# A22 T4 by Strassen once more in a convolution and hard-swish kernel, with its sums, signs and tiles rearranged

## Chip, core and metric

The kernel runs on one core of one Trainium2 chip. The metric is the device time of one execution, in microseconds; before the change it is 2399.19 us, the median of 3 runs (2398.7 to 2399.26).

## What is computed

```python
def _attn_ref(x, weight):                  # x (8, 4096, 192), weight (8, 7)
    w = softmax(weight, axis=-1)           # a weight for each head and tap
    x_pad = zeros of 6 rows in front of x
    out[b, s, h*24+g] = sum_k w[h, k] * x_pad[b, s + k, h*24+g]

def _moe_ref(x, w_in, w_out):              # w_in (192, 2048), w_out (2048, 192)
    h = x @ w_in
    relu6 = np.clip(h + 3.0, 0.0, 6.0)
    g = h * relu6 / 6.0
    return (g @ w_out).astype(np.float32)
```

The 8 x 4096 tokens that leave the causal convolution go through the two products; everything is float32 on the chip.

## The kernel before, in words

**Blocks.** The tokens are cut into 32 blocks of 1024, each of them two groups of N = 512 tokens. Block 0 is done plainly (`out_direct`), the last by `out_last`, and the 30 between by an h phase (`h_phase`) and an output phase (`out_strassen`). The loop stands at the end of the kernel. The order of the work on each engine is the order in the source (`manual_schedule`); every engine takes its own instructions in turn, and the waits between engines follow from the tiles that they read and write.

**Convolution.** Seven taps for a block's next neighbour, each one DVE instruction on 128 partitions x 1536 elements: the lower 64 partitions hold one token group, the upper 64 the other (`conv_units`, L271 the first tap, L275 the six others). They are issued at the start of the output phase. `swap` copies the halves across by two DMAs on SP (`OWN` and `OTHER` of tile `y`), and `y_sums` (L296) makes four sums for the Strassen form of the first product.

**h phase.** Four units of two halves. The plans `FIRST`, `SECOND` and `OTHERS` write out the order of PE's 88 matmuls (L323, 64 rows each; a float32 matmul is two instructions) and of the steps that follow: copies on ACT (L408, L411), the adds of p5 on DVE (L415, steps `AF` and `AD`), the relu on ACT (L329) and the gate on DVE (L333), which writes g. `X` in the first plan is the last store of the block before.

**g and its quarters.** g lies as A11, A21, A12, A22: half of the 2048 hidden features by token group. A11 and A12 are group 0, A21 and A22 group 1. After each unit POOL makes S3 = A11 - A21 (L517, 128x1024) and issues a DMA that adds A22 to A21 in place, which gives S1 (L443), and four sums of A11's quarters for the second level of Strassen (`a11_sums`, L537, 128x256 each, in tile `sums`).

**Output phase.** The seven products of Strassen's form (Winograd's variant, `prod`) are run in groups of four 32-column matmuls side by side, one PSUM bank to a group:

- `a11_round`: the first two 32-column pieces of A11 B11 by seven half products of 256 tokens (L545), beside its third piece and pieces of A12 B21 (L456). Two PSUM banks. Its results are put together by a copy on ACT and seven adds of 32x256 on DVE, with scratch tile `mp`.
- `three(4, 2, 1)`: A22 T4 (three pieces) and one of A12 B21.
- `rest_of_2` (L598): what is left of A12 B21, four matmuls of 512 tokens and four of 256.
- `three(7, 5, 0)`, `three(6, 5, 1)`, `three(3, 5, 2)`: S3 T3, S2 T2 and S4 B22, with the pieces of S1 T1.

Between them DVE has, in this order: the convolution's seven taps, the adds of `a11_round`, S2 = S1 - A11 in A11's place (L517, two instructions of 128x2048), the adds of the rest, S4 = A12 - S2 in A12's place (L517, two more), the sums of the results, transposes into `xt` (L647) and `y_sums`. SP stores the transposed rows and loads x for a later block. The six result tiles and `mp` (pool `cs`) and `xt` (pool `ot`, four buffers) have SBUF of their own. PSUM banks are taken and given back in turn (`take`, `give`).

**Weights.** At the start, POOL makes the sums of the weights (`w_sums`, L222), among them T1 to T4 of w_out and, in `w_q`, four sums of B11's quarters.

Of the kernel before, what the change touches and what calls it, by code (L numbers as in the profile page):

```python
# [16 lines left out]
def kernel(  # L17
# [7 lines left out]
):  # L25

# [127 lines left out]
    w_q = cst.tile([P, 4, UNITS, QS], F32, name="w_q")  # L154
# [64 lines left out]
    def w_sums():  # L219

        def sub(out, x, y):
            nc.gpsimd.tensor_tensor(out=out, in0=x, in1=y, op=ALU.subtract)  # L222

        for o, x, y in ((T1, B12, B11), (T3, B22, B12), (T2, B22, T1), (T4, T2, B21)):
            sub(w_out[:, :, o], w_out[:, :, x], w_out[:, :, y])
        y11, y12, y21, y22 = (
            w_out[:, c::2, B11, q * QS : (q + 1) * QS] for c in range(2) for q in range(2)
        )
        t1, t2, t3, t4 = (w_q[:, j] for j in range(4))
        for o, x, y in ((t1, y12, y11), (t3, y22, y12), (t2, y22, t1), (t4, y21, t2)):  # L230
            sub(o, x, y)
        b11, b12, b21, b22 = (w_in[:, c::2, s] for s in range(2) for c in range(2))
        t1, t2, t3, t4 = (w_in_t[:, j] for j in range(4))
        for o, x, y in ((t1, b12, b11), (t3, b22, b12), (t2, b22, t1), (t4, b21, t2)):
            sub(o, x, y)
# [24 lines left out]

    def conv_units(i, parts, cuts=1):


        x = x_tiles.pop(i)
        W = N // cuts

        def tap(part, k, t):
            c = c_sb[:, k : k + 1]
            to = y[:, part, t : t + W]
            if k == 0:  # L270
                nc.vector.tensor_scalar(  # L271
                    out=to, in0=x[:, part, t : t + W], scalar1=c, scalar2=None, op0=ALU.mult
                )
            else:
                nc.vector.scalar_tensor_tensor(  # L275
                    out=to, in0=x[:, part, k + t : k + t + W], scalar=c, in1=to,
                    op0=ALU.mult, op1=ALU.add,
                )

        return [  # L280
            lambda part=part, k=k, t=t: tap(part, k, t)
            for part in parts for k in range(KC) for t in range(0, N, W)
        ]
# [28 lines left out]
    def give(b):  # L312
        free_banks.append(b)
# [14 lines left out]
    def relu(r6, h):  # L328
        nc.scalar.activation(r6, h, ACT.Relu, bias=half[:], scale=1.0 / 6.0)  # L329
# [48 lines left out]
    class Unit:  # L378
# [7 lines left out]
        def run(self, op):  # L386
            u, k, bank = self.u, self.k, self.bank

            def slot(c, s):
                return w_in[:, 2 * u + c, s]  # L390

            mms = {
                "P1": ("a", slot(0, 0), OWN), "P2": ("a", slot(0, 1), OWN + 1),
                "K11": ("a", slot(0, 2), OWN + 2), "P5": ("e", w_in_t[:, 0, u], YS1),
                "P6": ("b", w_in_t[:, 1, u], YS2), "P7": ("b", w_in_t[:, 2, u], YS3),
                "P4": ("b", w_in_t[:, 3, u], OTHER + 1), "K21": ("b", slot(0, 2), OTHER + 2),
                "P3": ("f", slot(1, 1), YS4), "K12": ("f", slot(1, 2), OWN + 2),
                "K22": ("d", slot(1, 2), OTHER + 2),
            }
            if op in mms:  # L400
                to, w, third = mms[op]
                first = op in ("P1", "P5")
                if first:
                    bank[to] = take()
                half_mm(k, bank[to], w, third, first, True, not first)
            elif op == "F1":
                bank["b"] = take()
                nc.scalar.copy(out=psum[:, bank["b"]], in_=psum[:, bank["a"]])  # L408
            elif op == "CE":
                self.p5 = p5s.tile([P, N], F32, name="p5")  # L410
                nc.scalar.copy(out=self.p5[:], in_=psum[:, bank["e"]])  # L411
                give(bank["e"])
            elif op in ("AF", "AD"):
                to = bank[op[1].lower()] = take()
                nc.vector.tensor_tensor(  # L415
                    out=psum[:, to], in0=psum[:, bank["b"]], in1=self.p5[:], op=ALU.add
                )
            elif op[0] == "R":
                r6 = self.r6[op[1]] = rs.tile([P, N], F32, name="r6")
                relu(r6[:], psum[:, bank[op[1]]])  # L420
            else:
                group, c = self.results[op[1]]
                b = bank[op[1]]
                gate(g_of(2 * u + c, group, k), self.r6[op[1]][:], psum[:, b])
                give(b)

    def h_phase(left):
        work = {(u, k): Unit(u, k) for u in range(UNITS) for k in range(2)}
        for u, plan in enumerate(PLANS):
# [9 lines left out]
            if u:  # L439
                slots = slice(2 * u - 2, 2 * u)  # L440
# [5 lines left out]
            if u < UNITS:  # L446
                a11_sums(u)
# [32 lines left out]
    def out_direct(i, work):  # L480

        parts = [(k, q) for k in range(G) for q in range(G * NQ)]
        for r in range(0, len(parts), 4):
# [17 lines left out]
            xt = ot.tile([P, N], F32, name="xt")  # L501
            nc.vector.transpose(out=xt[:], in_=bank)
# [4 lines left out]
    def g_sums(engine, which, slots, width):  # L507

        forms = {
            3: (S3, A11, A21, ALU.subtract),  # L510
            2: (S2, S1, A11, ALU.subtract), 4: (S4, A12, S2, ALU.subtract),
        }
        for n in which:
            o, a, b, op = forms[n]
            for p in slots[::width]:
                r = slice(p, p + width)
                engine.tensor_tensor(out=o[:, r], in0=a[:, r], in1=b[:, r], op=op)  # L517

# [9 lines left out]
    X11, X12, X21, X22 = (A11[:, c::2, t : t + TH] for t in (0, TH) for c in range(2))  # L528

    def a11_sums(u):  # L530

        s1, s2, s3, s4 = (sums[:, n, u] for n in range(4))
        for o, a, b, op in (
            (s1, X21[:, u], X22[:, u], ALU.add), (s3, X11[:, u], X21[:, u], ALU.subtract),
            (s2, s1, X11[:, u], ALU.subtract), (s4, X12[:, u], s2, ALU.subtract),
# [17 lines left out]
    def a11_round(i, p1, p2):  # L553

        ba, bb = take(), take()
        a, b = (psum[:, n] for n in (ba, bb))
        y11, y12, y21, y22 = (
            w_out[:, k::2, B11, q * QS : (q + 1) * QS] for k in range(2) for q in range(2)
        )
        t1, t2, t3, t4 = (w_q[:, n] for n in range(4))  # L560
        s1, s2, s3, s4 = (sums[:, n] for n in range(4))
        m0 = (
            quarters(a, 0, first_half, X11, y11) + quarters(a, 0, second_half, X12, y21)
# [3 lines left out]
            quarters(a, 1, first_half, X22, t4)  # L567
            + quarters(a, 1, second_half, A12[:, ::2, first_half], w_out[:, ::2, B21, rows(2)])
            + quarters(b, 1, first_half, s1, t1) + quarters(b, 1, second_half, s4, y22)
        )  # L570
        m2, m3 = product(a, 2, 1, 2), product(a, 3, 2, 0)
        for n in range(NP):
            for mms, k in ((m0, 2 * n), (m1, 2 * n), (m2, n), (m3, n),
                           (m0, 2 * n + 1), (m1, 2 * n + 1)):
                mms[k]()
        mp = cs.tile([P, TH], F32, name="mp")
        r1, r2, r3 = (mp[rows(n)] for n in range(3))
        nc.scalar.copy(out=r1, in_=a[rows(0), first_half])
        piece(p1, 2, a, 2)
        piece(p2, 0, a, 3)  # L580
        add(p1[rows(0), first_half], r1, a[rows(0), second_half])
        add(r2, r1, b[rows(0), first_half])
        add(r3, r2, b[rows(0), second_half])
        add(p1[rows(0), second_half], r3, a[rows(1), first_half])
        add(p1[rows(1), second_half], r3, b[rows(1), first_half])
        add(r2, r2, b[rows(1), first_half])
        add(p1[rows(1), first_half], r2, b[rows(1), second_half])
# [3 lines left out]
    def rest_of_2(a):  # L591
# [3 lines left out]
        w = w_out[:, :, B21, rows(2)]  # L595
        for p, tokens in ((1, slice(0, N)), (0, second_half)):
            for j in range(4):
                nc.tensor.matmul(  # L598
                    out=bank[rows(j), tokens], lhsT=w[:, 2 * j + p],
                    rhs=A12[:, 2 * j + p, tokens], start=bool(p), stop=True,  # L600
                    tile_position=(0, j * QS), skip_group_check=True,
                )
# [40 lines left out]
    def store(i, c, k, half_, qs=range(NQ), queues=(nc.sync,), tokens=slice(0, N)):  # L643

        xt = ot.tile([P, N], F32, name="xt")
# [4 lines left out]

    def sums_tiles():
        return (cs.tile([DH, N], F32, name=f"c{k}") for k in range(6))
# [3 lines left out]
    def out_last(i):  # L656
# [19 lines left out]
        add(u2[:], p1[:], bank[m])  # L676
# [4 lines left out]
        add(p4[two], u3[two], p4[two], ALU.subtract)  # L681
# [7 lines left out]
        for t in range(0, N, N // 2):  # L689
# [9 lines left out]
            add(u3[rows(2), ts], u3[rows(2), ts], bank[rows(NQ), ts], ALU.subtract)  # L699
# [3 lines left out]
    def out_strassen(i, conv):  # L703
# [3 lines left out]
        ba, a = a11_round(i, p1, p2)  # L707
        g_sums(nc.vector, (2,), every, 4)
        b, bank = three(4, 2, 1)
        nc.scalar.copy(out=p4[:], in_=bank[m])  # L710
        piece(p2, 1, bank, NQ)
        give(b)
        swap(slice(0, K3))
        b, bank = rest_of_2(a)
        pieces(p2, 2, bank)
        give(b)
        add(p2[rows(2), first_half], p2[rows(2), first_half], a[rows(1), second_half])
        give(ba)
        g_sums(nc.vector, (4,), every, 4)
# [7 lines left out]
        add(u2[:], p1[:], bank[m])  # L727
# [3 lines left out]
        add(p4[:], u3[:], p4[:], ALU.subtract)  # L731
# [27 lines left out]
    with tc.manual_schedule():  # L759
# [115 lines left out]
        cs = ctx.enter_context(tc.tile_pool(name="cs", bufs=1))  # L875
        ot = ctx.enter_context(tc.tile_pool(name="ot", bufs=4))
# [8 lines left out]
        sums = ss.tile([P, 4, UNITS, N // 2], F32, name="sums")  # L885
        left = []
        for i in range(1, NB):
            h_phase(left)
# [39 lines left out]
```

## Time and profile before

| | |
|---|---|
| runs, median of 3 | 2399.19 us |
| the profiled execution | 2398.86 us |
| its span, first to last instruction | 2397.1 us |
| busy: PE | 2388.7 us (100%) |
| busy: DVE | 2138.0 us (89%) |
| busy: ACT | 1087.9 us (45%) |
| busy: POOL | 836.4 us (35%) |
| granted TensorE clock | 1.000 |
| PE L323 (h) | 884.8 + 524.5 us |
| PE L456, L545, L598 (products of the output phase) | 1120.0 + 218.9; 109.4 + 108.5 and two smaller forms; 31.6 and one smaller |
| DVE L275 (six taps), mean of one | 1786 ns over all shapes; 1922 ns for 128x1536 |
| DVE L271 (first tap), 128x1536 | 1806 ns |
| POOL L537 (sums of A11's quarters) | 188.1 + 101.9 + 90.3 us, 728 to 831 ns each |
| POOL L517 (S3) | 293.8 us, 2369 ns each |
| POOL's DMAs (L443) | 124 of 512 KB, 5.0 us from issue to landing |

A table of groups gives, for each source line and shape, how often it ran, for how long in all, and what the engine was waiting for before it. The order in time gives start, length, engine, line, operation, tiles and, in brackets, the idle time ahead. PE is TensorE's matmuls, PEld its weight loads, DVE is VectorE, ACT ScalarE, POOL GpSimd, SP the engine that issues most DMAs. PE's busy time is the union of overlapping matmuls, so the matmuls of one line share it with those beside them. Times within a block below are microseconds from the start of the span, in the block whose h phase runs from 1133.61 to 1171.83 and whose output phase from 1171.83 to 1207.62.

### The profile page before, as it was taken

Reading aid. Unit: us, or ns where it says so; the run is one execution under the profiler, and the core shown is the slowest. Engines: PE = TensorE matmul, PEld = TensorE weight load, DVE = VectorE, ACT = ScalarE, POOL = GpSimd, SP = SyncE. Lnnn points to the kernel's source line nnn. Section 1 sums busy time; section 2 is a strip of 40 time slices with the busy share of each in tenths; the row PEclk is TensorE's granted clock in tenths of the full one; section 3 lists DMA queues with packets and bytes.
Section 4 is the critical chain, followed back from the end, with each engine's and each line's share of the span. In section 5 each row is a group of like instructions: output and inputs, shape, how many; then the busy total and the mean of one; then the engine's idle time right before and its main releaser. Section 6 shows DMA issues by size and latency. Waiting matters only on the chain.

```text
span 2397.1 us, 43036 instructions
## 1 busy us (share of the span) xinstructions
PE 2388.7 (100%) x17496; PEld 1105.0 (46%) x17496; DVE 2138.0 (89%) x2773; ACT 1087.9 (45%) x1858; POOL 836.4 (35%) x780
## 2 busy tenths in 40 slices
PE   9999999999999999999999999999999999999998
PEld 6444444444444444444454444444444444444443
DVE  8798889988899988899888998889998889988896
ACT  7234553345543355433454334553445543455433
POOL 2524432234422344223443224432234422344222
PEclk9999999999999999999999999999999999999999
DMA  5233333323333233333333333333323233333322
GB/s 146 46 56 64 62 61 64 67 50 69 59 59 66 53 73 60 60 58 57 67 63 58 67 57 59 63 67 58 67 52 73 54 65 59 55 70 63 58 51 43
DMA packets 261143, 149.86 MB, mean 63 GB/s; under 512 B 207504, under 2 KB 212624, under 8 KB 260944
## 3 DMA queue, kind: packets, MB, share of 16 engines
q1 hardware_dynamic: 225880, 81.56, 16.9%
q0 software_dynamic: 33824, 65.28, 15.8%
q8 instruction: 137, 2.24, 0.4%
q14 instruction: 62, 0.51, 0.1%
q10 hardware_dynamic: 1240, 0.27, 0.1%
HBM read 31.72 MB, written 25.17 MB: 24 GB/s over the span
## 4 chain that ended last, share of the span: by engine, by line
PE 99%; DMA 0%; DVE 0%; SPq 0%; ACT 0%; issue 0%; DVEq 0%; ACTq 0%
PE psum L323 51%; PE psum L456 41%; PE psum L545 5%; PE psum L598 2%; DMA x<-in_x_dram 0%; DMA out_dram<-xt 0%; DVE c L641 0%; DVE xt L647 0%; SPq L106 0%; SPq L140 0%; DVE top L184 0%; PE psum L774 0%; DVE y L275 0%; SPq L95 0%; ACT y L788 0%
## 5 line engine op out<-in xcount | busy, mean ns | idle before, releaser
L456 PE MATMUL psum<-g,w_out 128*32 128x512 f32 (+1 forms) x7936 | 1120.0, 589 | 0.0
L323 PE MATMUL psum<-y,w_in 64*128 64x512 f32 x3664 | 884.8, 591 | 0.4 <-DVE y L275 0.3
L329 ACT ACTIVATE r<-psum,half 128x512 f32<-128x512 f32 x1024 | 641.0, 688 | 241.6 <-PE psum L323 234.8
L333 DVE SCALAR_TENSOR_TENSOR g<-r,psum 128x512 f32<-128x512 f32 x1024 | 641.7, 681 | 4.7 <-ACT r L329 1.5
L323 PEld LDWEIGHTS psum<-y,w_in 64*128 64x128 f32 x3664 | 441.6, 187 | 362.6 <-issue 292.2
L537 POOL TENSOR_TENSOR sums<-g 128x256 f32<-128x256 f32 x248 | 188.1, 831 | 1181.3 <-DVE g L333 1163.2
L456 PEld LDWEIGHTS psum<-g,w_out 128*32 128x32 f32 x7936 | 339.4, 110 | 460.3 <-issue 438.1
L323 PE MATMUL psum<-y,w_in_t 64*128 64x512 f32 x1984 | 524.5, 593 | 0.0
L415 DVE TENSOR_TENSOR psum<-psum,p 128x512 f32<-128x512 f32 x496 | 324.5, 694 | 193.1 <-PE psum L323 184.7
L633 ACT COPY c<-psum 32x512 f32<-32x512 f32 x218 | 126.0, 578 | 588.2 <-PE psum L456 571.0
L517 POOL TENSOR_TENSOR s<-g 128x1024 f32<-128x1024 f32 x124 | 293.8, 2369 | 245.5 <-PE psum L323 237.7
L275 DVE SCALAR_TENSOR_TENSOR y<-x,c_sb,y 128x1536 f32<-128x1536 f32 (+1 forms) x206 | 366.5, 1786 | 6.6
L323 PEld LDWEIGHTS psum<-y,w_in_t 64*128 64x128 f32 x1984 | 247.7, 186 | 195.2 <-issue 124.9
L517 DVE TENSOR_TENSOR g<-g 128x2048 f32<-128x2048 f32 x124 | 279.5, 2296 | 7.4 <-DMA g<-g 3.9
L456 PE MATMUL psum<-s,w_out 128*32 128x512 f32 x1488 | 218.9, 592 | 0.0
L408 ACT COPY psum<-psum 128x512 f32<-128x512 f32 x248 | 138.8, 571 | 71.7 <-PE psum L323 56.1
L443 POOL DMA_DIRECT2D g<-g x124 | 149.1, 1202 | 39.8 <-POOL s L517 39.8
L641 DVE TENSOR_TENSOR c<-c,psum 32x512 f32<-32x512 f32 (+2 forms) x219 | 139.8, 638 | 16.0 <-ACT c L633 9.7
L411 ACT COPY p<-psum 128x512 f32<-128x512 f32 x248 | 133.2, 591 | 41.1 <-PE psum L323 40.3
L456 PEld LDWEIGHTS psum<-s,w_out 128*32 128x32 f32 x1488 | 70.8, 110 | 129.2 <-issue 124.8
L545 PE MATMUL psum<-g,w_out 128*32 128x256 f32 x720 | 109.4, 380 | 0.0
L545 PE MATMUL psum<-sums,w_q 128*32 128x256 f32 x720 | 108.5, 379 | 0.0
(64 smaller groups left out, 1080.1 us busy)
## 6 DMA issues: line engine op xcount, KB each, us to landing
g<-g POOLq DMA_DIRECT2D x124, 512.0 KB, 5.0
out_dram<-xt SPq DMA_DIRECT2D x380, 64.0 KB, 2.0
y<-y SPq DMA_DIRECT2D x62, 384.0 KB, 4.7
x<-in_x_dram SPq DMA_DIRECT2D x55, 388.5 KB, 6.0
stage<-in_moe_w_in_dram SPq DMA_DIRECT2D x16, 192.0 KB, 4.4
stage<-in_moe_w_out_dram SPq DMA_DIRECT2D x8, 384.0 KB, 5.1
x<-in_x_dram SPq DMA_DIRECT2D x7, 384.0 KB
y<-y SPq DMA_DIRECT2D x6, 128.0 KB, 2.4
```

The lines of the kernel that those rows point to most:

```text
L275: nc.vector.scalar_tensor_tensor(out=to, in0=x[:, part, k + t : k + t + W], scalar=c, in1=to, op0=ALU.mult, op1=ALU.add,)
L323: nc.tensor.matmul(out=psum[:, b], lhsT=w[r], rhs=y[r, third_of_y], start=start, stop=stop, skip_group_check=onto,)
L329: nc.scalar.activation(r6, h, ACT.Relu, bias=half[:], scale=1.0 / 6.0)
L333: nc.vector.scalar_tensor_tensor(out=out, in0=r6, scalar=1.0, in1=h, op0=ALU.min, op1=ALU.mult)
L408: nc.scalar.copy(out=psum[:, bank["b"]], in_=psum[:, bank["a"]])
L415: nc.vector.tensor_tensor(out=psum[:, to], in0=psum[:, bank["b"]], in1=self.p5[:], op=ALU.add)
L443: nc.gpsimd.dma_start(out=S1[:, slots], in_=A22[:, slots], accum_op=ALU.add)
L456: lambda p=p: nc.tensor.matmul(out=bank[j * QS : (j + 1) * QS, tokens], lhsT=w_out[:, p, w, cols], rhs=x[:, p, tokens], start=(first and p ...
L517: engine.tensor_tensor(out=o[:, r], in0=a[:, r], in1=b[:, r], op=op)
L537: nc.gpsimd.tensor_tensor(out=o, in0=a, in1=b, op=op)
L545: lambda u=u: nc.tensor.matmul(out=dst[rows(j), tokens], lhsT=w[:, u], rhs=x[:, u], start=(u == 0 and tokens == first_half), stop=(u == UN ...
L641: nc.vector.tensor_tensor(out=out, in0=x, in1=y, op=op)
```

## The change

- **Products.** `a11_round` becomes `round_twice(n, ...)`, called twice: for A11 B11, and for A22 T4, whose first two pieces now go by seven half products as well. It takes the place of `three(4, 2, 1)`; its third piece and a piece of A12 B21 run beside it. The even half of A12 B21's last piece, second 256 tokens, moves into the second round, so `rest_of_2` keeps only its four 512-token matmuls.
- **Sums.** `quarter_sums(n, u)` makes for A22, too, four sums of 128x256 a unit on POOL; those of unit u - 1 stand ahead of that unit's S3 and S1 DMA. The last block makes none. `w_q` holds four more weight sums, of T4's quarters.
- **Signs.** The convolution's weights of group 1 are negated (`c_sg`), so h, A21 and A22 are; the relu of that group has scale -1/6. S3, S2 and S4 become sums, T1 changes sign, and some later adds and subtractions swap.
- **S2.** Since it is now a sum, its slots 0 to 3 are made by two adding DMAs from POOL; DVE makes slots 4 to 7 in one instruction.
- **First tap.** For every block but block 0 it is a multiplication on ACT.
- **Tiles.** Two tiles of 8 slots x 512 hold the sums of A11 and of A22; the six result tiles, `mp` and the four `xt` lie in slots of them.

```diff
         def tap(part, k, t):
-            c = c_sb[:, k : k + 1]
+            c = (c_sg if i else c_sb)[:, k : k + 1]
             to = y[:, part, t : t + W]
-            if k == 0:
+            if k == 0 and i:
+                nc.scalar.mul(to, x[:, part, t : t + W], c)
+            elif k == 0:
...
+        for n, block in enumerate((B11, T4)):
+            y11, y12, y21, y22 = (
+                w_out[:, c::2, block, q * QS : (q + 1) * QS]
+                for c in range(2) for q in range(2)
+            )
+            t1, t2, t3, t4 = (w_q[:, n, j] for j in range(4))
+            for o, x, y in ((t1, y12, y11), (t3, y22, y12), (t2, y22, t1), (t4, y21, t2)):
+                sub(o, x, y)
...
             if u:
+                if twice:
+                    quarter_sums(1, u - 1)
                 slots = slice(2 * u - 2, 2 * u)
                 g_sums(nc.gpsimd, (3,), range(NP)[slots], 2)
 
                 nc.gpsimd.dma_start(
                     out=S1[:, slots], in_=A22[:, slots], accum_op=ALU.add
                 )
-            if u < UNITS:
-                a11_sums(u)
+            if u < UNITS and twice:
+                quarter_sums(0, u)
...
-        mp = cs.tile([P, TH], F32, name="mp")
-        r1, r2, r3 = (mp[rows(n)] for n in range(3))
+        mp = tile_at(0, 2, P)
+        r1, r2, r3 = (mp[rows(k), first_half] for k in range(3))
...
+    def quarter_sums(n, u):
+
+        x11, x12, x21, x22 = (x[:, u] for x in quarter[n])
+        s1, s2, s3, s4 = (sums[n][:, j, u] for j in range(4))
         for o, a, b, op in (
-            (s1, X21[:, u], X22[:, u], ALU.add), (s3, X11[:, u], X21[:, u], ALU.subtract),
-            (s2, s1, X11[:, u], ALU.subtract), (s4, X12[:, u], s2, ALU.subtract),
+            (s1, x21, x22, ALU.add), (s3, x11, x21, ALU.subtract),
+            (s2, s1, x11, ALU.subtract), (s4, x12, s2, ALU.subtract),
         ):
             nc.gpsimd.tensor_tensor(out=o, in0=a, in1=b, op=op)
...
-    def rest_of_2(a):
+    def rest_of_2():
...
-        w = w_out[:, :, B21, rows(2)]
-        for p, tokens in ((1, slice(0, N)), (0, second_half)):
-            for j in range(4):
...
+        for j in range(4):
+            nc.tensor.matmul(
+                out=bank[rows(j)], lhsT=w_out[:, 2 * j + 1, B21, rows(2)],
+                rhs=A12[:, 2 * j + 1], start=True, stop=True, tile_position=(0, j * QS),
+            )
...
+    def tile_at(n, k, parts):
+        return sums_at[n][0:parts, k]
...
     def sums_tiles():
-        return (cs.tile([DH, N], F32, name=f"c{k}") for k in range(6))
+        return (tile_at(n, k, DH) for n, k in ((0, 0), (0, 1), (1, 0), (1, 1), (1, 2), (1, 3)))
+
+    xt_slots = [4, 6, 5, 7]
+
+    def next_xt():
+        xt_slots.append(xt_slots.pop(0))
+        return tile_at(1, xt_slots[-1], P)
...
-        ba, a = a11_round(i, p1, p2)
-        g_sums(nc.vector, (2,), every, 4)
-        b, bank = three(4, 2, 1)
-        nc.scalar.copy(out=p4[:], in_=bank[m])
-        piece(p2, 1, bank, NQ)
-        give(b)
+        ba, a = round_twice(0, first_half, p1, (1, 2, p1), (2, 0, p2))
+
+        for slots in (slice(0, 2), slice(2, 4)):
+            nc.gpsimd.dma_start(out=S2[:, slots], in_=S1[:, slots], accum_op=ALU.add)
+        g_sums(nc.vector, (2,), range(4, NP), 4)
+        bb, b = round_twice(1, second_half, p4, (4, 2, p4), (2, 1, p2))
         swap(slice(0, K3))
-        b, bank = rest_of_2(a)
+        b2, bank = rest_of_2()
         pieces(p2, 2, bank)
-        give(b)
-        add(p2[rows(2), first_half], p2[rows(2), first_half], a[rows(1), second_half])
+        give(b2)
+        for bank, tokens in ((a, first_half), (b, second_half)):
+            add(p2[rows(2), tokens], p2[rows(2), tokens], bank[rows(1), second_half])
         give(ba)
+        give(bb)
         g_sums(nc.vector, (4,), every, 4)
```

## Prediction

> **What bounds the kernel now.** I read first the page's chain that ended last (its shares by engine), then the busy times in the two stages of one steady block.
>
> ```profile
> PE 99%; DMA 0%; DVE 0%; SPq 0%; ACT 0%; issue 0%; DVEq 0%; ACTq 0%
> ...
> 1133.61:1171.83 38.22, 38.22 (x181) 21.91 (x177) 32.09 (x53) 27.73 (x47) 20.00 (x20) 1.00 0.36 66
> 1171.83:1207.62 35.79, 35.79 (x371) 13.50 (x369) 35.02 (x35) 5.68 (x11) 5.59 (x5) 1.00 0.30 57
> ```
>
> The columns of the last two lines are stretch, length, then PE, PEld, DVE, ACT, POOL busy. The first stretch is the h phase, the second the output phase; a block is 74 us, and there are 30 such blocks. PE never stops, so PE time saved is time saved. But in the output phase DVE is busy 35.02 of 35.79 us: it is a second bound, hidden only by its order. So I looked at when DVE delivers what PE needs. First DVE in the output phase, then PE's pieces of the block before (same lengths) from the chain in order of time:
>
> ```profile
> 1173.85 1.81 DVE L271 TENSOR_SCALAR y<-x,c_sb 128x1536 f32<-128x1536 f32 x1
> 1175.70 11.49 DVE L275 SCALAR_TENSOR_TENSOR y<-x,c_sb,y 128x1536 f32<-128x1536 f32 x6
> ...
> 1190.17 4.49 DVE L517 TENSOR_TENSOR g<-g 128x2048 f32<-128x2048 f32 x2
> ...
> 1197.31 4.50 DVE L517 TENSOR_TENSOR g<-g 128x2048 f32<-128x2048 f32 x2
> ...
> 1104.92 6.87 PE psum L456 x64
> 1111.79 1.29 PE psum L598 x16
> 1113.08 20.60 PE psum L456 x192
> ```
>
> The last L517 line is S4. Its first half ends at 1199.6 (half of 4.50 after 1197.31). The output phase ends at 1207.62, and its last product group (S4 by B22, the last third of the 20.60) takes PE 6.87, so it starts at 1200.75. S4 has 1.15 us to spare, and everything that DVE does after the h phase (seven taps, adds, S2, adds, S4) is queued ahead of it. That is the number on which this change turns.
>
> Third, POOL around the end of that h phase:
>
> ```profile
> 1167.15 2.35 POOL L517 TENSOR_TENSOR s<-g 128x1024 f32<-128x1024 f32 x1 [2.67 <-PE psum L323]
> 1169.80 1.20 POOL L443 DMA_DIRECT2D g<-g  x1 [0.30 <-POOL s L517]
> 1170.91 1.53 POOL L537 TENSOR_TENSOR sums<-g 128x256 f32<-128x256 f32 x2
> 1172.29 0.84 POOL L537 TENSOR_TENSOR sums<-sums,g 128x256 f32<-128x256 f32 x1
> 1173.21 0.73 POOL L537 TENSOR_TENSOR sums<-g,sums 128x256 f32<-128x256 f32 x1
> 1173.90 2.39 POOL L517 TENSOR_TENSOR s<-g 128x1024 f32<-128x1024 f32 x1
> 1177.28 1.20 POOL L443 DMA_DIRECT2D g<-g  x1 [0.98 <-POOL s L517]
> ```
>
> In each 9.45 us unit of the h phase POOL idles only about 2.7 us (the bracket), and its last S3 already reaches into DVE's taps. What that costs a tap (the first of these lines), and what POOL's weight sums at the start cost (the others):
>
> ```profile
> 1175.70 2.22 DVE L275 SCALAR_TENSOR_TENSOR y<-x,c_sb,y 128x1536 f32<-128x1536 f32 x1
> 1177.95 1.82 DVE L275 SCALAR_TENSOR_TENSOR y<-x,c_sb,y 128x1536 f32<-128x1536 f32 x1
> ...
> 70.58 3.27 DVE L275 SCALAR_TENSOR_TENSOR y<-x,c_sb,y 128x1536 f32<-128x1536 f32 x1
> 67.10 1.82 POOL L222 TENSOR_TENSOR w_out<-w_out 128x768 f32<-128x768 f32 x1
> 68.88 3.34 POOL L222 TENSOR_TENSOR w_out<-w_out 128x768 f32<-128x768 f32 x1
> ...
> 80.50 1.90 DVE L275 SCALAR_TENSOR_TENSOR y<-x,c_sb,y 128x1536 f32<-128x1536 f32 x1
> 84.72 0.46 POOL L222 TENSOR_TENSOR w_q<-w_out,w_q 128x128 f32<-128x128 f32 x1
> ```
>
> A tap is 1.82 us alone, 3.27 us beside 768-element POOL sums (which go from 1.82 to 3.34), 1.90 us beside 128-element ones. They take turns.
>
> **What the Trainium skill says.** "SBUF — State Buffer", section "SBUF: two separate sides": GpSimd and a DVE op with two SBUF inputs share a port pair as an exclusive lock held for the whole instruction; the loser blocks. The trace agrees: 3.27 against 1.82 us. Gates (one input in PSUM) are the same 0.68 us with or without POOL. "ScalarE: Activation LUTs", section "What ACT_TABLE_LOAD costs": 280 ns + 0.833 ns an element with a pointer operand, so 1.56 us for the moved tap; from the trace 1.59 us (a 128x512 one of the same kind is 0.723 us, and ACT copies of 256 and 512 elements, 361 and 578 ns, give 0.85 ns an element). "DMA: Bandwidth & Descriptors", section "SWDGE vs HWDGE vs iDMA": an accumulating DMA can only be issued from GpSimd, which is why S2's two stand behind POOL's sums.
>
> **The change, part by part.** All in the clock of this block.
>
> *Products (PE).* A22 T4's first two column pieces go by seven half products: the second round replaces the group of 6.87 us, and the four 256-token matmuls leave the remainder, 1.29 x 2/3 = 0.86, saves 0.43. Do 256-wide matmuls pay? In the round of today the 512-wide pairs beside them come every 0.429 us (16 pairs, 1172.30 to 1178.73 for 15 steps), as in the plain group (6.87/16): no; I take 0.02. Saved 0.41 us a block; at worst the round's whole excess of today, 7.03 - 6.87 = 0.16, comes again, and 0.27 is saved. On the path: 30 x 0.41 = 12.3 us.
>
> *A22's sums (POOL).* 4 units x 4 sums, 2.99 us a unit (1170.91 to 1173.90), into 2.7 us of idle: POOL falls behind. Walked from the first sum of the block (1142.63) with no idle left (units of 2.99 + 2.99, S3 and its DMA 3.79), A11's last sums end at 1174.8 instead of 1173.9. Then A22's last four and S3 (6:8) are still to come, 5.35 us of POOL's own time, all beside DVE's taps. Price of one on a tap: its own time less 0.37 (1.82 costs 3.27 - 1.82 = 1.45; 0.46 costs 0.08). So 4 x (0.72 - 0.37) + (2.36 - 0.37) = 3.4 us, against 0.40 today. Ends: 0.4 (nothing new; A22's sums then slip between) and 5.35 (all of it).
>
> *First tap on ACT.* ACT's last relu ends at 1173.2; 1.59 us; so tap 1 starts at about 1174.9, not 1175.70: DVE gains 0.80, not 1.81. The moved tap read one SBUF operand and was not held up by POOL; what moves forward is a tap that is. ACT is idle there (5.68 busy of 35.79): free. The new wait, tap 1 for ACT, has all of DVE's output phase queued behind it. Ends 0.6 to 0.95.
>
> *S2.* Half by DVE leaves 2.25 us of 4.49. The two DMAs stand on POOL behind S3 and the last S1 DMA: taps 1 to 4 with a sum each end near 1183.7, S3 near 1185.8, S1's DMA 0.98 later at 1186.8, landing (median 5.0) 1191.8; S2's follow at 1188.0 and 1189.2, landing 1193.0 and 1194.2, or 1194.8 and 1197.8 if each must take its 3.0 us alone (15.8% of 2397 us by 126 DMAs). Product 6 wants the first at 1193.5. DVE's own half of S2 waits for S1's landing (1191.8) and stands behind the conv, which ends at 1187.15 - 0.80 + 3.0 (the taps' loss, above) = 1189.4, and the first round's adds, 1192.4: no wait.
>
> *Adds (DVE).* Seven 256-adds as in round one, 3.04 us (the adds of L641 between the last tap at 1187.10 and S2 at 1190.17), and one more, 0.44. They share one scratch tile, so ACT's copy for the second round waits until DVE has read the first's (1192.4); behind it on ACT stand only copies that DVE wants later, and no relu for 15 us. SP's queue: the swap starts with the conv's end, 1189.5 instead of 1187.25, and lands 4.7 later, long before y_sums (after 1206): nothing.
>
> *The rest:* w_sums' four more small sums lie in the start, where POOL idles 18 us afterwards: nothing. Signs: nothing (same instructions). Result tiles in the sums' slots: each store's DMA lands in 2.0 us, the slot is written again over 20 us later: nothing. w_q and c_sg: two tiny instructions. PSUM banks: eight taken in turn, each given back before its next use.
>
> **The sum.** S4's first half: 1199.60 - 0.80 - 2.25 + 3.04 + 0.44 = 1200.03, with today's 0.40 of port loss; with 3.4, 1203.0. PE wants it at 1200.75 - 0.41 = 1200.34. So PE waits 2.7 (0.1 more for the signal) before its last group. The S1 and S2 landings lie under that wait: even 1197.8 for slots 2 and 3 puts the end of product 6 at 1197.8 + 6 x 0.86 = 1203.0. Next is late: DVE's first p5 add in the next h phase ends 12.16 us after S4's first half (1199.60 to 1211.76); PE needs it at its twelfth step, 6.87 + 11 x 0.433 = 11.6 us after it started that group. Another 0.5. A block: -0.41 + 2.8 + 0.5 = +2.9; x 30 = +87 on the profiled execution's 2398.86 us (span 2397.1; median of the runs 2399.19, 0.3 above): **2485**.
>
> **The rivals.** *Faster:* the port costs little, S4 comes in time, PE keeps 12.3 us: 2386.6. It decides at 0.3 us of port loss above today's 0.40 (1200.34 - 1200.03); with 0.7 gain and wait cancel. For it: total DVE work falls by under a microsecond. Against: 3.27 us taps in this very trace. *Slower still:* S2's landings, beside the swap's two DMAs at 1189.5 (4.7 us each), come 2 us later than 1197.8 and hold product 6: 2 x 30 more, 2545. *Doesn't do what it says:* if the second round costs the full 0.16, the gain is 8 us and the forecast 2489. *Milder:* if POOL keeps up and only S3 with one or two sums meets the taps (loss 2.0 to 2.4), the wait is 1.3 to 1.7 and the time 2440 to 2455.
>
> **Chances.** The DVE wait, its mild form and the full 0.16 included, 0.76 (2435 to 2520); late DMAs 0.08 (2520 to 2560); beyond 0.03; gain 0.10 (2386 to 2394); within 0.2% (4.8 us, about what can be told from no change) 0.03. Range 2435 to 2560 holds 0.84. Faster 0.10, same 0.03, slower 0.87.
>
> **What would show it.** Right: taps of about 2.4 us on average ((6 x 1.82 + 3.4)/6) instead of 1.92; PE waiting some 80 us in all for DVE's g (L517) at the product lines; blocks of 76.8 us; POOL without its 2.7 us brackets in the h phase. Wrong: taps still at 1.9; PE without waits; or PE waiting for the DMA on g.

## The result, and the profile after

The changed kernel takes **2643.84 us** (median of 4 runs, 2639.25 to 2649.55) against 2399.2 us, a ratio of 1.1021 [1.1, 1.1043]. The profiled execution took 2643.16 us (span 2641.3), granted clock 0.964. It is slower, as forecast, but by 245 us instead of 86, beyond the upper end of the range (2560).

Line numbers have moved: the products' matmuls are now L474, the second rounds L567, the six taps L290 and the moved tap L284, S3, S2 and S4 L535, POOL's quarter sums L559, S1's DMA L461, S2's DMAs L743, the swap L303 and L304. First the chain that ended last, by engine, of the kernel after:

```profile
PE 55%; POOL 24%; DMA 17%; issue 2%; DVE 2%; SPq 0%; POOLq 0%; ACT 0%; DVEq 0%; ACTq 0%
```

PE had 99% of it. Now 41% goes through POOL and DMAs, and DVE, which I had named as the bound to come, has 2%. Next the windows of one block: its h phase, its output phase, and two stretches within the latter (columns as in the prediction; the third number from the end is PE's granted clock, then the DMA share and GB/s):

```profile
1166.44:1204.52 38.08, 38.08 (x181) 20.33 (x177) 30.97 (x50) 27.79 (x47) 27.37 (x31) 1.00 0.33 60
1204.52:1250.13 45.61, 39.38 (x394) 15.43 (x392) 38.22 (x42) 7.51 (x13) 19.26 (x13) 0.93 0.42 73
1226.20:1236.00 9.80, 4.32 (x22) 0.92 (x26) 8.43 (x14) 0.58 (x1) 0.00 (x0) 0.81 0.89 162
1236.00:1243.30 7.30, 7.30 (x60) 1.99 (x56) 7.23 (x8) 0.00 (x0) 0.00 (x0) 0.79 0.12 19
```

The h phase is nearly what it was. The output phase is 45.61 instead of 35.79 us, and two things stand in it that no block of the kernel before had: 9.8 us in which PE is busy for 4.32 while the DMA engines are 89% busy, and a granted clock below 1. The mean block is 82.0 us (38.1 and 43.9) against 73.9.

The same output phase on DVE, POOL, PE, and then the DMA issues between 1218 and 1240 (the last number there is the median from issue to landing):

```profile
1207.38 14.51 DVE L290 SCALAR_TENSOR_TENSOR y<-x,c_sg,y 128x1536 f32<-128x1536 f32 x6 [0.76 <-ACT y L284]
...
1226.22 2.29 DVE L535 TENSOR_TENSOR g<-g 128x2048 f32<-128x2048 f32 x1 [1.30 <-DMA g<-g]
...
1235.56 4.49 DVE L535 TENSOR_TENSOR g<-g 128x2048 f32<-128x2048 f32 x2 [1.03 <-DMA g<-g]
```

```profile
1207.50 4.50 POOL L559 TENSOR_TENSOR sums<-g 128x256 f32<-128x256 f32 x2
...
1216.38 3.88 POOL L535 TENSOR_TENSOR s<-g 128x1024 f32<-128x1024 f32 x1
1220.57 1.20 POOL L461 DMA_DIRECT2D g<-g  x1 [0.30 <-POOL s L535]
1221.31 2.92 POOL L743 DMA_DIRECT2D g<-g  x2
```

```profile
1233.52 16.68 PE L474 MATMUL psum<-g,w_out 128*32 128x512 f32 x128 [5.48 <-DMA g<-g]
```

```profile
g<-g POOLq DMA_DIRECT2D x3, 512.0 KB, 12.2
y<-y SPq DMA_DIRECT2D x2, 384.0 KB, 8.6
```

DVE's taps take 14.51 us instead of 6 x 1.82 = 10.92, so they lose 3.6; the forecast was 3.4. POOL comes to S2's DMAs at 1221.31 and, by the trace, 1222.04, 16.8 and 17.5 us after the h phase; the forecast was 16.2 and 17.4. What is not as forecast is the landing. The first S2 DMA lands at 1233.5, 12.2 us after its issue, and PE stands 5.48 us for it. The second lands at 1235.5, and DVE's S4 waits 1.03 us for it. S1's last DMA, S2's two and the swap's two (SP issues them at 1221.95 and 1222.50) are in flight together. Over the whole run the waits of PE's products read (us in total, times, the longest):

```profile
PE psum L474 <- DMA g<-g: 167.2, 59, 6.1
```

That is 5.6 us a block; for DVE's g, where I expected 80 us, there is none.

The block above is one of seven in which POOL comes to the S2 DMAs at 16.8 us and they land within 2.4 us of each other. In 22 of the 30 blocks they leave about 2 us sooner, and PE stands twice, once for each of them, as here, where the output phase starts at 793.26:

```profile
818.27 2.73 PE L474 MATMUL psum<-g,w_out 128*32 128x512 f32 x16 [3.29 <-DMA g<-g]
823.25 13.60 PE L474 MATMUL psum<-g,w_out 128*32 128x512 f32 x112 [2.24 <-DMA g<-g]
```

In the mean of the 30 blocks the S2 DMAs are issued 15.4 and 16.1 us after the h phase and land at 25.9 and 30.2. After these waits PE runs at half clock in every block, for 3.41, 6.83 or 10.24 us (in one block twice 3.41), and the output phases last 41.9 to 45.6 us.

**Theory** after this reading: POOL's lateness makes S1 and S2 leave when the swap leaves; the five transfers share the 16 DMA engines; PE stands for S2, and the standing brings the half clock. **Rivals:** POOL's locks on DVE (my forecast) are the real cause and the DMA wait only covers it; the moved tap; S2 by DMA in itself; the second level of Strassen in itself.

### The profile page after: what moved, and what is told of

Its sections match the earlier page's. It is cut to its first block, busy times and chain, and to the rows that moved or that the text cites. A ratio compares the mean times of both kernels' runs of the same rounds, so it can differ in the third digit from the quotient of the medians.

```text
span 2641.3 us, 45785 instructions
## 1 busy us (share of the span) xinstructions
PE 2466.8 (93%) x18216; PEld 1162.5 (44%) x18216; DVE 2207.1 (84%) x2954; ACT 1144.1 (43%) x1919; POOL 1421.6 (54%) x1308
## 3 DMA queue, kind: packets, MB, share of 16 engines
q10 hardware_dynamic: 1240, 0.27, 0.1%
## 4 chain that ended last, share of the span: by engine, by line
PE 55%; POOL 24%; DMA 17%; issue 2%; DVE 2%; SPq 0%; POOLq 0%; ACT 0%; DVEq 0%; ACTq 0%
PE psum L338 32%; PE psum L474 21%; DMA g<-g 16%; POOL sums L559 14%; POOL s L535 7%; POOL g L461 2%; PE psum L567 2%; DMA out_dram<-sums 1%; DVE psum L430 1%; POOL g L743 1%; DVE g L348 0%; DVE sums L663 0%; PE psum L621 0%; DMA x<-in_x_dram 0%; SPq L493 0%
## 5 line engine op out<-in xcount | busy, mean ns | idle before, releaser
L474 PE MATMUL psum<-g,w_out 128*32 128x512 f32 (+1 forms) x6976 | 1200.8, 633 | 167.2 <-DMA g<-g 167.2
L559 POOL TENSOR_TENSOR sums<-g 128x256 f32<-128x256 f32 x480 | 434.3, 1005 | 1022.6 <-DVE g L348 1006.3
L474 PEld LDWEIGHTS psum<-g,w_out 128*32 128x32 f32 x6976 | 309.2, 115 | 621.9 <-issue 330.8
L290 DVE SCALAR_TENSOR_TENSOR y<-x,c_sg,y 128x1536 f32<-128x1536 f32 x186 | 444.6, 2390 | 29.8 <-ACT y L284 24.4
L655 ACT COPY sums<-psum 32x512 f32<-32x512 f32 x248 | 143.3, 578 | 698.5 <-PE psum L474 695.2
L663 DVE TENSOR_TENSOR sums<-sums,psum 32x256 f32<-32x256 f32 (+1 forms) x669 | 323.8, 487 | 123.5 <-ACT sums L655 104.6
L535 POOL TENSOR_TENSOR s<-g 128x1024 f32<-128x1024 f32 x124 | 338.6, 2730 | 53.5 <-DVE g L348 39.7
L535 DVE TENSOR_TENSOR g<-g 128x2048 f32<-128x2048 f32 x94 | 212.8, 2291 | 55.2 <-DMA g<-g 52.8
L559 POOL TENSOR_TENSOR sums<-sums,g 128x256 f32<-128x256 f32 x240 | 257.2, 1072 | 0.0
L559 POOL TENSOR_TENSOR sums<-g,sums 128x256 f32<-128x256 f32 x240 | 217.0, 904 | 18.8
L474 PE MATMUL psum<-s,w_out 128*32 128x512 f32 x1488 | 221.5, 592 | 0.0
L567 PE MATMUL psum<-g,w_out 128*32 128x256 f32 x1440 | 218.1, 380 | 0.0
L567 PE MATMUL psum<-sums,w_q 128*32 128x256 f32 x1440 | 217.0, 379 | 0.0
L461 POOL DMA_DIRECT2D g<-g x124 | 149.1, 1202 | 40.1 <-POOL s L535 39.2
```

What stands on the lines that cost most here:

```text
L290: nc.vector.scalar_tensor_tensor(out=to, in0=x[:, part, k + t : k + t + W], scalar=c, in1=to, op0=ALU.mult, op1=ALU.add,)
L461: nc.gpsimd.dma_start(out=S1[:, slots], in_=A22[:, slots], accum_op=ALU.add)
L474: lambda p=p: nc.tensor.matmul(out=bank[j * QS : (j + 1) * QS, tokens], lhsT=w_out[:, p, w, cols], rhs=x[:, p, tokens], start=(first and p ...
L559: nc.gpsimd.tensor_tensor(out=o, in0=a, in1=b, op=op)
L567: lambda u=u: nc.tensor.matmul(out=dst[rows(j), tokens], lhsT=w[:, u], rhs=x[:, u], start=(u == 0 and tokens == first_half), stop=(u == UN ...
L655: nc.scalar.copy(out=dst[rows(q)], in_=src[rows(j)])
```

## The experiments

**Everything but the second level.** A22 T4 goes by the plain group again, without A22's sums, and the remainder of A12 B21 is as in the kernel before; signs, first tap on ACT, S2's half by DMA and the shared tiles stay.

```diff
-                if twice:
-                    quarter_sums(1, u - 1)
...
-        bb, b = round_twice(1, second_half, p4, (4, 2, p4), (2, 1, p2))
+        b, bank = three(4, 2, 1)
+        nc.scalar.copy(out=p4, in_=bank[m])
+        piece(p2, 1, bank, NQ)
+        give(b)
```

> The changed kernel without the second level for A22 T4: no A22 sums, the product group and the remainder of the kernel before; the signs, the first tap on ACT, half of S2 by two adding DMAs and the shared tiles stay. Theory A: these cost nothing, since S2's DMAs start at the first round's end and land before the swap: 2399 plus or minus 4. Rival B: S2's DMAs land late here too, PE waits for them: above 2450.

Measured: **2399.13 us**, 0.9999 [0.9991, 1.0008]. With none of A22's sums on POOL, the four rearrangements together cost nothing. The whole 245 us come with the second level and what it makes late.

**POOL's sums put into the kernel before.** The kernel before, with A22's 16 sums a block added on POOL, into slots of S3 that S3 overwrites next; nobody reads them.

```diff
+                a22_sums(u - 1)
```

> The kernel before, with A22's sixteen quarter sums a block made on POOL in the place where the change makes them, into slots of S3 that S3 overwrites next; nobody reads them. Theory A: the lock alone. Taps lose 3 us more a block (mean about 2.4 us), S4's first half comes 3.0 us later against 1.15 us to spare, so PE waits 1.9 us for DVE and 0.5 us more in the next h phase: 2399 + 30 x 2.4 = about 2470 us, PE's clock full[...]. If POOL's sums cost DVE nothing: 2399. Rival B (S2's DMAs are the whole loss): 2399 to 2405.

Measured: **2470.5 us**, 1.0297 [1.0282, 1.0313]. PE's wait in this kernel:

```profile
PE psum L457 <- DVE g L518: 35.4, 30, 1.5
```

So the price of POOL's locks is real, and the expectation for this run was met: 71 us, through the late S4 (1.2 us of waits a block, in an output phase that is 1.7 us longer; and a later start of the next h phase's p5 adds, which makes that phase 38.83 instead of 38.11 us in the mean), with the clock at 1.000. It is not what the changed kernel shows.

**The swap left out.** y's other half then keeps old values in 30 output phases.

```diff
         bb, b = round_twice(1, second_half, p4, (4, 2, p4), (2, 1, p2))
-        swap(slice(0, K3))
```

> The changed kernel without the swap's two DMAs in the 30 output phases (the other token half of y stays old, so h is not the reference's). Theory A with the DMA engines shared: S2's two DMAs follow S1's at 3 us each, land about 5 us earlier, PE's wait for them falls[...], its clock stays full, and the wait for S4 behind DVE (2.8 to 3.8 us in all) takes over: 2490 to 2530. If the swap doesn't matter to S2's DMAs: about 2640.

Measured: **2488.92 us**, 1.0374 [1.0357, 1.0391], blocks of 76.9 us in the mean, clock 0.999. One block of it (h phase ending at 1062.58): its DMAs, DVE's S4, and the waits of all blocks:

```profile
g<-g POOLq DMA_DIRECT2D x3, 512.0 KB, 7.3
```

```profile
1091.15 4.49 DVE L535 TENSOR_TENSOR g<-g 128x2048 f32<-128x2048 f32 x2
```

```profile
PE psum L474 <- DMA g<-g: 45.9, 61, 2.1
PE psum L474 <- DVE g L535: 13.7, 22, 0.8
```

Without two transfers of 384 KB the median of the three adding DMAs is 7.3 instead of 12.2 us from issue to landing in these blocks; in the mean of 30 blocks S2's two take 7.5 and 9.6 us instead of 10.5 and 14.2, and land at 22.4 and 25.2 us after the h phase, close to the later of the forecast's two cases, 23.0 and 26.0. The waits of PE fall from 167 to 60 us, and all but one stretch of half clock in the steady blocks go. That is the forecast's number (2485, blocks of 76.8), and S4 is as late as forecast: its first half ends 1091.15 + 2.25 - 1062.58 = 30.8 us after the h phase; the forecast put it at 1203.0 - 1171.83 = 31.2. But the forecast had all of PE's wait for DVE's g, and here 45.9 of 59.6 us are waits for S2's DMAs, so that the total agrees so well is in part luck.

**The swap later.** The same two DMAs, issued from ACT's queue after S3 T3's group, with all the work done.

```diff
-        swap(slice(0, K3))
...
         b7, bank7 = three(7, 5, 0)
         piece(p5, 0, bank7, NQ)
+        swap(slice(0, K3), nc.scalar)
```

> The changed kernel with the swap's two DMAs issued from ACT's queue, after its copy of the first piece of S1 T1: 5 us later or more, behind S2's DMAs; nothing is left out. Theory A (S2's DMAs lose their time to the swap, which lies between them in the shared DMA engines): as without the swap, 2489 plus or minus 8, PE's clock full. If it is the amount of DMA work in the output phase that counts and not its order: about 2640.

Measured: **2491.95 us**, 1.0385 [1.037, 1.0401], clock 0.998. PE's waits:

```profile
PE psum L474 <- DMA g<-g: 59.8, 60, 2.8
PE psum L474 <- DVE g L535: 5.8, 21, 0.4
```

A move of two DMAs by 4.5 us takes 152 us off; the clash, not the transfers, was the cost. The queue changes with the time here, but the run without the swap is only 3 us below this one, so the queue can have little part in it.

**PE kept busy during the wait.** 24 matmuls that nobody uses, ahead of the group that waits for S2, into the bank that this group overwrites.

```diff
+        for n in range(24):
+            nc.tensor.matmul(
+                out=psum[rows(n % 4), free_banks[0]], lhsT=w_out[:, 0, B21, rows(0)],
+                rhs=S3[:, 0], start=True, stop=True, tile_position=(0, n % 4 * QS),
+            )
         b, bank = three(6, 5, 1)
```

> The changed kernel with 24 idle matmuls (128x512, four side by side, 24 x 0.2147 = 5.15 us at the full clock) ahead of the product group that waits for S2's DMAs, into the PSUM bank that this group then overwrites: PE stands for about 0.4 instead of 5.5 us, everything else is as it was. If PE's half clock after the wait comes from standing still, the records show the clock near 1.0, a block loses its 2.9 us of half clock (82.0 to about 79.1) and the time is 2557 us (2545 to 2580). If the half clock comes from what goes on at the same time (four large transfers, DVE and POOL busy), it stays, and the time stays at 2644 or goes above it, to 2660. If the idle matmuls themselves only push the rest back, up to 2700.

Measured: **2606.47 us**, 1.0858 [1.084, 1.0876], clock 0.999. One block on PE (the idle matmuls are L761), and its output phase in the windows:

```profile
1208.97 5.74 PE L761 MATMUL psum<-s,w_out 128*32 128x512 f32 x45
1215.06 14.21 PE L474 MATMUL psum<-g,w_out 128*32 128x512 f32 x128 [0.35 <-DMA g<-g]
```

```profile
1186.04:1229.20 43.16, 42.01 (x443) 16.67 (x441) 38.23 (x42) 7.50 (x13) 19.26 (x13) 1.00 0.41 73
```

The half clock comes from standing still: the DMAs are as slow as before (S2's two land at 26.05 and 30.43 us after the h phase in the mean, against 25.88 and 30.24), yet the clock is 1.00. But it is worth 37 us, not the 87 that I had expected. At full clock PE comes sooner to the slots of the second S2 DMA, which lands 4.4 us after the first in the mean, and waits there (47.4 us of waits for these DMAs are left). Most of the half clock was under a wait in any case.

**The order on POOL.** A22's sums behind S3 and the S1 DMA of each unit instead of ahead of them.

```diff
-                if twice:
-                    quarter_sums(1, u - 1)
...
                 nc.gpsimd.dma_start(
                     out=S1[:, slots], in_=A22[:, slots], accum_op=ALU.add
                 )
+                if twice:
+                    quarter_sums(1, u - 1)
```

> The changed kernel with each unit's A22 sums behind its S3 and its S1 DMA on POOL instead of ahead of them. Theory A: the last S1 DMA goes out about 10 us earlier, S2's two about 2 us earlier with nothing ahead of them, so they land before or with the swap; the taps still lose 3.0 us to POOL, so PE waits 2.7 us for S4 behind DVE and 0.8 us in the next h phase: 2485 to 2505, clock full. If S2's landing is bound by the swap alone: about 2640.

Measured: **2639.06 us**, 1.0999 [1.0983, 1.1016]; 134 us above what I expected at most. PE's first wait in the block whose h phase ends at 1203.77:

```profile
1211.73 0.41 PE L567 MATMUL psum<-sums,w_q 128*32 128x256 f32 x2 [2.60 <-POOL sums L559]
```

```profile
PE psum L567 <- POOL sums L559: 153.5, 60, 3.6
```

I had looked at one end of the row only. A22's sums of each unit now stand ahead of A11's of the next, so PE waits for the sums themselves, 153.5 us in 60 waits, clock 0.973. The number that I had given for the rival (2640) is met by chance: PE's waits for DMAs on g are 1.1 us in this run. With either order POOL is late; the order chooses what PE waits for.

**The first tap back on DVE.**

```diff
-            if k == 0 and i:
-                nc.scalar.mul(to, x[:, part, t : t + W], c)
-            elif k == 0:
+            if k == 0:
```

> The changed kernel with the first tap on DVE as before. Its one SBUF input was not held up by POOL, so POOL gets 1.8 us in which to run two or three of A22's last sums beside it; S3 and the DMAs behind it come 2 to 3 us earlier. Theory A: PE's wait for S2's DMAs falls[...]: 2480 to 2540, so the moved tap cost more than it saved. If the tap's 1.8 us on DVE count instead: slower than 2644 by up to 30 us.

Measured: **2537.5 us**, 1.0578 [1.0561, 1.0596]: the tap moved to ACT costs 106 us. POOL beside that tap, which runs from 1157.24 to 1159.05 here:

```profile
1158.20 1.43 POOL L557 TENSOR_TENSOR sums<-g 128x256 f32<-128x256 f32 x2
```

The tap with one SBUF input is the one stretch among DVE's taps in which POOL's sums run without turns: these two took 4.50 us in the changed kernel's block above. With it, S2's DMAs leave 2.3 us sooner in the mean of 30 blocks, 4.8 us ahead of the swap instead of 2.0, and PE's waits for DMAs on g fall from 167 to 70 us.

**S2 all on DVE,** without S2's DMAs.

```diff
-        for slots in (slice(0, 2), slice(2, 4)):
-            nc.gpsimd.dma_start(out=S2[:, slots], in_=S1[:, slots], accum_op=ALU.add)
-        g_sums(nc.vector, (2,), range(4, NP), 4)
+        g_sums(nc.vector, (2,), every, 4)
```

> The changed kernel with all of S2 on DVE, as before, and no S2 DMAs. Theory A: DVE, held up by POOL, becomes the one to wait for: S2 two instructions after S1's landing, S4 at 34 us after the h phase instead of 28.5: PE waits 1.8 us before product 6 and 3.8 us before the last group, and 0.8 us in the next h phase: 2580, or up to 2630 where the second wait halves the clock. Rival B (S2's DMAs are the loss): 2485 or less.

Measured: **2571.78 us**, 1.0722 [1.0706, 1.0738]. PE now waits 124.5 us for DVE's g and 4.4 for DMAs. Even 2.25 us more on DVE are cheaper than two late DMAs in the clash; against the kernel with the later swap they are dearer by 80 us.

**A22's sums only in the first block.** The products of A22 T4 then read whatever lies in the sums' slots (the results and `xt` are put there, too).

```diff
-                if twice:
+                if twice == 2:
...
-            h_phase(left, i + 1 < NB)
+            h_phase(left, 2 if i == 1 else i + 1 < NB)
```

> The changed kernel, but POOL makes A22's quarter sums in the first of the 30 blocks only; the second round then multiplies old sums, so the products' values are not the reference's. Theory A (A22's sums on POOL hold up DVE's taps, and push POOL's S1 and S2 DMAs behind the conv, where they share the DMA engines with the swap; the long wait then halves PE's clock): all of it goes, S2's DMAs start at the first round's end, and PE keeps the saved products: about 2388 us. Rival B (adding DMAs into A11 land late wherever they are issued): still above 2600. Rival D (the second round is slower on PE than the group that it replaces): above 2399.

Measured: **2436.99 us**, 1.0158 [1.0143, 1.0173]; I had expected 2388, the products' full gain. POOL's S3 runs from 1122.19 to 1124.58 here; DVE's first tap in that output phase, and PE's waits:

```profile
1122.98 3.21 DVE L290 SCALAR_TENSOR_TENSOR y<-x,c_sg,y 128x1536 f32<-128x1536 f32 x1 [0.76 <-ACT y L284]
```

```profile
PE psum L474 <- DVE g L535: 14.7, 29, 0.5
```

With the first tap on ACT the next tap moves forward into S3's lock and takes 3.21 us instead of 1.82. S4's first half ends 29.0 us after the h phase, PE needs it at 28.4, and the next h phase is 0.7 longer. So even without a single sum of A22 the second level has no room on DVE for its 3.5 us of adds.

**Later swap and tap on DVE together,** the two best single steps.

```diff
-            if k == 0 and i:
-                nc.scalar.mul(to, x[:, part, t : t + W], c)
-            elif k == 0:
+            if k == 0:
...
-        swap(slice(0, K3))
...
         piece(p5, 0, bank7, NQ)
+        swap(slice(0, K3), nc.scalar)
```

> The changed kernel with the swap issued after the first transposed-sum group as in the run with the later swap (2492 us), and with the first tap back on DVE (which alone brought 2644 to 2538). Theory: with the swap out of the way what is left is DVE's own row of work. The tap back on DVE brings S2's DMAs about 1 us forward and ends PE's 2.0 us a block of waiting for them, but S4's first half ends at +31.7 us after the h phase (as in the run with the tap on DVE) against PE's need at +28.5; PE waits 3.2 us for it and 0.5 more in the next h phase, less the 0.41 saved: 2399 + 30 x 3.3 = 2498 us (2488 to 2508), no better than the later swap alone. Rival: PE's wait for the DMAs is the only thing between the later-swap kernel and the time before; then it falls by 60 us, to about 2432.

Measured: **2516.66 us**, 1.0489 [1.0474, 1.0505]. PE's waits:

```profile
PE psum L472 <- DVE g L533: 67.8, 30, 3.0
PE psum L472 <- DMA g<-g: 15.5, 16, 2.0
```

The rival (2432) falls: with the DMAs out of the way S4 is the bound, as in the forecast, and the tap is wanted on ACT again. It is 18 us above what I expected: in 14 of the 30 blocks a wait was followed by half clock, mostly for 3.41 us (output phases of 40.3 beside 38.4 us). Waits of the same length in other blocks brought none; what decides is in the last section. No version here beats the kernel before.

## Why the prediction was wrong

By the runs, in order of what was put back (2399.2 before, 2492.0 with the later swap, 2606.5 with PE kept busy, 2643.8 after), the loss is 93 + 115 + 37 us (the middle term includes whatever the idle matmuls add themselves, and another order could divide it otherwise). The forecast was 86.

- **POOL's sums on DVE's taps: right,** 3.6 us for 3.4, down to the single instruction: taps beside one sum took 2.17 or 2.18 us (1.82 + 0.35), the one beside S3 3.82 (1.82 + 2.0). 128x1536 taps average 2.39 us; forecast 2.4.
- **First tap on ACT: right in time,** wrong in weight. It took 1.57 us in the mean (forecast 1.59; the 1.56 in the prediction was an estimate from the skill's figure) and DVE waits 0.8 for it. What failed is the word "free". The moved tap was POOL's only free stretch among the taps; moving it put POOL's DMAs 2.3 us later, which here cost 106 us.
- **S4 and the p5 adds: right in how late they come** (30.8 us for 31.2 without the swap; the next h phase 0.7 us longer for a forecast of 0.5). The total of +2.9 us a block, against 76.9 - 73.9 = 3.0 without the swap, is in part luck, since most of PE's waits there are for S2's DMAs. As PE's main wait S4 is seen in the kernel before with A22's sums (35.4 us) and in the run with the later swap and the tap on DVE (67.8).
- **S2's DMAs: the step that failed.** The issues were right within 0.6 us in the block shown and 0.8 to 1.3 us early in the mean. The landings were put at +21.2 to +26.0 us after the h phase, and "The S1 and S2 landings lie under that wait". They came at +25.9 and +30.2 in the mean (+29.0 and +31.0 in the block shown). I let S2's DMAs compete with each other only, which is right without the swap (+22.4 and +25.2). The swap was in the sum as "lands 4.7 later, long before y_sums (after 1206): nothing", because I asked what its own reader needs and not what it takes from the transfers beside it. In "slower still" I had the right mechanism, at 2 us and 0.08; its price is about 115/30 = 3.8 us a block even when PE is kept busy. The prediction's own formula says the same: with +30.2 for the second landing, product 6 ends at 30.2 + 6 x 0.86 = 35.4 instead of 31.2 us after the h phase, an estimate of 4.2 us a block or 126 us; with the forecast's 86 and the half clock's 37 that is 249, for the 245 measured.
- **Missing: the half clock.** No term of the sum had it. The Trainium skill has it, in "TensorE: Matmul & The Clock Gate", section "HAM oscillation — how this bites in real kernels": PE that stands through a window of about 3.4 us falls to half clock, and a DMA wait in every round of a loop pays this each time. The trace agrees on the loop (stretches of 3.41 us and multiples in each of the 30 blocks), but not on the length: mostly it took two waits of 1.2 to 3.7 us. It is 37 us here. I had not asked what such waits bring in their train.
- **The products: right.** In the block shown the second round starts at 1211.42, the remainder at 1218.29 and the next group at 1219.15: 6.87 us, as the group that it replaces, and 0.86 instead of 1.29. So 0.43 us a block are saved on PE (forecast 0.41), and the medians of the 30 blocks say the same; the rival that the second round is slow on PE falls.
- **What would show it:** taps at 2.4 us and POOL without its idle brackets came true; "PE waiting for the DMA on g" was named as the sign against, and that is what stands in the waits.

Not tried: S3 by an adding DMA instead of a POOL sum, which would shorten POOL's row by some 1.2 us a unit (2.37 of the sum against 1.20 of an issue); more bytes in the same DMA engines speak against it, and more than the products' 12 us below the kernel before could not come of it.

## What to carry to other kernels

When an engine that issues DMAs falls behind, work out not only when its transfers leave but what else is in flight at that time, and price a landing by all their bytes together. An instruction moved off a contended engine may have been the breathing space of a third one: look at who runs freely beside it. Waits of PE that leave it idle for about 2 us within a few microseconds can have a second price, the half clock after them, and it is worth trying to move a bulk transfer out of the stretch before touching the arithmetic.

## What the runs showed of the hardware

- **One pool for all queues.** Of three adding DMAs of 512 KB from POOL in a row, the second and third take 7.5 and 9.6 us in the mean without the swap, and 10.5 and 14.2 us beside the swap's 2 x 384 KB from SP. The Trainium skill says so in "DMA: Bandwidth & Descriptors", section "Issuing engines are not separate DMA queues": DMAs from any queue end on the same 16 engines and interleave. The traffic was 162 GB/s in the crowded stretch.
- **Idle time in a window of 3.41 us, not the length of one wait, brings the half clock.** In each run the stretches of half clock start on a fixed grid of 3.41 us: all 32 of the changed kernel lie at the same place in it within 2 ns. I cut the nine traces that have such stretches in their steady blocks into the windows of this grid, without the first 60 and the last 20 us. PE, by the records of its matmuls, was idle for 1.98 us or more in each of the 133 windows at full clock that were followed by half clock, and for at most 2.03 us in all others at full clock. The half clock went on after windows with 0.79 us of idle time or more and ended after those with 0.77 or less. So a wait of 2.32 us brought it in the run with PE kept busy, and one of 3.63 us, which lay across two windows, did not in the run with the tap on DVE. The section of the skill named beside the half clock above speaks of gaps over about 3.4 us; these traces say about 2.0 us within one window, and the measurement decides.
- **A POOL operation costs a DVE operation with two SBUF inputs 0.35 us** (128x256 sum of 0.73 us alone) or 2.0 us (128x1024 sum of 2.37 us alone), and one POOL operation gets in per DVE operation.
